# Grouped-query attention and a gated MLP: a fifth query buffer, fourth batch's query loads together, first v in halves

## The chip, the cores and the metric

The kernel runs on one core of a Trainium2 chip. The metric is the device time of one launch in microseconds: the median of several runs. A profiled execution gives the trace that the text reads; its span runs from the first to the last instruction. Engines: PE (TensorE), DVE (VectorE), ACT (ScalarE), POOL (GpSimd), SP (SyncE, here used for DMA issues alone).

## The reference

```python
B, Hq, Hkv, S, D = 8, 16, 4, 384, 64        # x is then B x 384 x 1024
k = np.repeat(k, 4, axis=1); v = np.repeat(v, 4, axis=1)
scores = np.matmul(q, k.transpose(0, 1, 3, 2)) / np.sqrt(D)
attn = softmax(scores)
x = np.matmul(attn, v).transpose(0, 2, 1, 3).reshape(B, S, 1024)

h = np.maximum(x @ w_in, 0.0)               # w_in 1024 x 1024
u, v = h[..., :512], h[..., 512:]
v_n = (v - mean(v)) / np.sqrt(var(v) + 1e-06)
v_s = np.einsum('ts,bsd->btd', w_spatial, v_n) + b_spatial[None, :, None]
out = (u * v_s) @ w_out                     # w_out 512 x 1024, out float32
```

All inputs are float32; the matmuls run in float16.

## The kernel before

The work is cut into 8 batches. A batch's attention has 18 units (`UNITS`): 6 sets (`SETS`, three tiles of 128 queries by two halves `j` of the heads) of 3 key tiles each. A unit's scores are two matmuls into PSUM (`units`, L277), ACT takes their exponential (`exp`, L289), and when a set's three units are through, PE multiplies with v (`weigh`, L297) and DVE divides by the row sums (L310, L312). The gated MLP of a batch follows behind as filler: `v_part` (L352), `u_part` (L411), the norm of v on POOL (`norm`, L396, results called vn), the spatial mixing `s_part` (L430, with DVE L442 and POOL L447), and `o_part` (L468, output stored by SP, L483). A generator (`gated`) hands it out matmul by matmul, with marks ("from", n) before which a part may not start; `pour` puts so much of it between the attention's units as a budget allows.

The order on each engine is that in which the program writes its instructions; the framework adds semaphore waits and nothing is reordered. A table `todo`, filled by `at(n, f, ...)`, calls loads, casts and transposes at unit n (the first 21 units are walked one by one, later ones three at a time: 21, 24, ... 36, 39, ...). So SP's queue is one list in program order: an instruction that waits holds all that stand behind it.

For each batch, q comes in two halves of 8 heads (`load_q`, L122, 768 KB each), k and v in one load each (`load_k`, `load_v`, L112, 384 KB). They land in float32 stage tiles from the pool `ld`: 4 rotating buffers for q (6 KB per partition each), 2 each for k and v. A tile's new load waits until the last reader of the tile that had the buffer before is done. POOL casts them to float16 (`cast_q` L200 to L205, `cast_k` L184, `cast_v` L188). For batches 0 and 1, PE transposes q and k (`q_turn` L237, `k_turn` L223); from batch 2 on, DMA does (`q_send` L255, `k_send` L247, results qT and kT), as it does for x (`x_send` L336, result xt, three sends per batch). PE reads qT and kT in the scores and xt in `v_part` and `u_part`.

At the start batch 0's loads are cut into parts that are spread over SP's and ACT's DMA queues (L141 to L149); `part_q(0, j, hs, ts, eng)` loads tiles `ts` of q's half `j`. A DMA's completion is told by one of 8 semaphores in rotation, so each SP or ACT load also waits until the one eight before it has landed. The third tiles follow later (`rest_q`). POOL casts v (`cast_v`, L585), issues weight loads and the loads of batch 1 (L586 to L592). The spatial weights and bias, `ws32` and `b32`, are constants of their own (L525, L526), loaded by SP (`load_spatial`), cast by POOL (`cast_spatial`) and transposed by DMA (L547).

From batch 3 on the same table rows serve each batch (L653 to L667), with two offsets `late` for batch 3. There the first q half is loaded at unit 38, the second at 40 (a step later); they are cast at 43 and 47 and transposed at 47 and 49.

Of the kernel before, what the change touches and what calls it, by code (L numbers as in the profile page):

```python
# [9 lines left out]
FP32 = mybir.dt.float32  # L10
# [7 lines left out]
def kernel(  # L18
# [15 lines left out]
    P = 128  # L34
    B, HQ, S, D = q.shape
    HKV = k.shape[1]
# [3 lines left out]
    NT = S // P  # L40
# [7 lines left out]
    UNITS = NT * SETS  # L48
# [4 lines left out]
    cst = ctx.enter_context(tc.tile_pool(name="cst", bufs=1))  # L53
    ld = ctx.enter_context(tc.tile_pool(name="ld", bufs=2))
# [12 lines left out]
            name=nc.get_next_instruction_name(), act_func_set_id=set_id, ins=[], outs=[]  # L67
        )
    )
    pool, dve, act, sp = nc.gpsimd, nc.vector, nc.scalar, nc.sync  # L70
# [32 lines left out]
    def stage_tile(n, b, j=None):  # L103
        shape = [P, 2, NT, G * D] if n == "q" else [P, HKV, NT * D]
        t = ld.tile(
            shape, FP32, name=f"{n}32_{b}_{j}", tag=f"{n}32", bufs=4 if n == "q" else 2
        )
        stage[n, b, j] = t
        return t

    def part(src, t, lo, hi, eng):
        eng.dma_start(t[:, lo:hi, :], src[lo:hi].rearrange("h (p t) d -> p h (t d)", t=NT))  # L112

    def load_k(b, eng=sp):
        part(k[b], stage_tile("k", b), 0, HKV, eng)

    def load_v(b, eng=sp):
        part(v[b], stage_tile("v", b), 0, HKV, eng)

    def part_q(b, j, hs, ts, eng):  # L120
        h0, h1, t0, t1 = hs[0], hs[-1] + 1, ts[0], ts[-1] + 1
        eng.dma_start(  # L122
            stage["q", b, j][:, h0:h1, t0:t1],
            q[b, 8 * j + 4 * h0 : 8 * j + 4 * h1].rearrange(
                "(h i) (c t r) d -> (i c) h t (r d)", i=G, t=NT, r=G
            )[:, :, t0:t1],
        )

    def load_q(b, j, eng=sp, ts=(0, 1, 2)):
        if ts[0] == 0:  # L130
            stage_tile("q", b, j)
        part_q(b, j, (0, 1), ts, eng)

    k0, v0, q00, q01 = (
        stage_tile("k", 0),
        stage_tile("v", 0),
        stage_tile("q", 0, 0),
        stage_tile("q", 0, 1),
    )
# [4 lines left out]
    part_q(0, 0, (1,), (0,), act)  # L144
    part(k[0], k0, 2, 4, sp)
    part_q(0, 1, (0, 1), (0,), act)
    part(v[0], v0, 0, HKV, sp)
    part_q(0, 0, (0, 1), (1,), act)
    part_q(0, 1, (0, 1), (1,), sp)  # L149

    w_in16 = cst.tile([P, NK, DFF], FP16, name="w_in16")
    w_out16 = cst.tile([P, NM, DM], FP16, name="w_out16")
# [5 lines left out]
    def load_w_in(half, lo, hi):  # L158
        cols = slice(half * DH, (half + 1) * DH)
        pool.dma_start(  # L160
            w_in16[:, lo:hi, cols],
            moe_w_in[lo * P : hi * P, cols].rearrange("(t p) f -> p t f", p=P),
        )
# [15 lines left out]
    def cast_k(b, eng, js=(0, 1), hs=slice(0, 2)):  # L179
        if b not in k16s:  # L180
            k16s[b] = ld.tile([P, 2, NT, 2, D], FP16, name=f"k16_{b}", tag="k16")
        src = stage["k", b, None].rearrange("p (j h) (t d) -> p j t h d", h=2, t=NT)
        for j in js:
            eng.tensor_copy(k16s[b][:, j, :, hs], src[:, j, :, hs])  # L184

    def cast_v(b, eng, js=(0, 1)):
        g0, g1 = 2 * js[0], 2 * js[-1] + 2
        eng.tensor_copy(  # L188
            v1[b % 2][:, g0:g1, :, 0:D].rearrange("p g t d -> p (g t) d"),
            stage["v", b, None][:, g0:g1].rearrange("p g (t d) -> p (g t) d", t=NT),  # L190
        )

    def cast_q(b, j, eng, ts=None, hs=(0, 1)):
        if (b, j) not in q16s:
            q16s[b, j] = ld.tile([P, NT, G, 2, D], FP16, name=f"q16_{b}_{j}", tag="q16", bufs=4)
        t16 = q16s[b, j]
        src = stage["q", b, j].rearrange("p h t (r d) -> p h t r d", d=D)
        for hh in hs:
            if ts is None:
                eng.tensor_copy(t16[:, :, :, hh, :], src[:, hh])  # L200
            elif len(ts) > 1:
                t = slice(ts[0], ts[-1] + 1)
                eng.tensor_copy(t16[:, t, :, hh, :], src[:, hh, t])
            else:
                eng.tensor_copy(t16[:, ts[0], :, hh, :], src[:, hh, ts[0]])  # L205
# [316 lines left out]
                yield from o_part(B - 1, tt, half)  # L522


    b32 = cst.tile([P, S], FP32, name="b32")  # L525
    ws32 = cst.tile([P, NT, S], FP32, name="ws32")  # L526
    ws16 = cst.tile([P, NT, NT, P], FP16, name="ws16")

    def load_spatial(eng):
        eng.dma_start(b32, moe_b_spatial.rearrange("(a s) -> a s", a=1).to_broadcast([P, S]))  # L530
        rows = moe_w_spatial.rearrange("(c t r) s -> r c t s", t=NT, r=G)
        for r in range(G):
            eng.dma_start(ws32[32 * r : 32 * r + 32], rows[r])

    def cast_spatial():
        pool.tensor_copy(
            bias_bc.rearrange("a (t r c) -> a t r c", t=NT, r=G),
            b32.rearrange("a (c t r) -> a t r c", t=NT, r=G),
        )
        for tt in range(NT):  # L540
            pool.tensor_copy(
                ws16[:, :, tt].rearrange("p s (r c) -> p s r c", r=G),
                ws32[:, tt].rearrange("p (c s r) -> p s r c", s=NT, r=G),
            )

    def send_spatial():
        sp.dma_start_transpose(  # L547
            wsT16.rearrange("p s (t c) -> p (s t) c", t=NT),
            ws16.rearrange("p s t c -> p (s t c)"),
        )  # L550
# [4 lines left out]
    def at(n, f, *args):  # L555
        todo.setdefault(n, []).append((f, args))
# [25 lines left out]
    q_turn(0, 0, 0, dve)  # L582
    idle(5)

    cast_v(0, pool)  # L585
    load_w_in(1, 4, 8)  # L586
    cast_q(0, 1, pool, (1,))
    load_k(1, pool)
    load_q(1, 0, pool)
    def behind_rest():  # L590
        load_q(1, 1, pool)
        load_v(1, pool)  # L592
        cast_q(0, 1, pool, (2,))
        load_w_in(0, 0, 4)
        load_w_in(0, 4, 8)
        pool.memset(b32[:, 0:1], 0.0)
        pool.memset(ws32[:, 0, 0:1], 0.0)
        load_spatial(sp)
        cast_k(1, pool)
        load_k(2, pool)  # L600
        cast_q(1, 0, pool)
        load_q(2, 0, pool, (0,))
        cast_q(1, 1, pool, (0,))
        cast_q(1, 1, pool, (1, 2))
        load_q(2, 1, pool, (0,))
        cast_v(1, pool)
        cast_spatial()
        send_spatial()

    at(3, behind_rest)  # L610
    at(2, idle, 6)
    at(2, cast_q, 0, 1, dve, (0,))
# [37 lines left out]
    for j, n in ((0, 34), (1, 36)):  # L650
        at(n, cast_q, 2, j, pool, (1, 2))
        at(n + 1, q_send, 2, j, 1, NT)
    for b in range(3, B):  # L653
        u0 = UNITS * b
        late = 6 if b == 3 else 0
        at(u0 - 24 + late, load_k, b)
        at(u0 - 24 + 2 * late, load_v, b)
        at(u0 - 22 + late, load_q, b, 0)
        at(u0 - 20 + late, load_q, b, 1)
        late = 3 if b == 3 else 0  # L660
        at(u0 - 16 + late, cast_k, b, pool)
        at(u0 - 14 + late, cast_q, b, 0, pool)
        at(u0 - 12 + late, k_send, b)
        at(u0 - 10 + late, q_send, b, 0)
        at(u0 - 10 + late, cast_q, b, 1, pool)
        at(u0 - 8 + late, q_send, b, 1)
        at(u0 - 4, cast_v, b, pool)  # L667

    STEP = (NT * NK * C512 + NM * NK * C384 + NM * NT * C384 + 6 * NM * C512) / SETS
# [48 lines left out]
    late = [(b, s, hh) for u in (ALONE, ALONE + 1) for b, s in ends.pop(u, []) for hh in range(2)]  # L718
    for n in range(ALONE, total, NT):
# [16 lines left out]
        late = []  # L736
# [41 lines left out]
```

## Time and profile before

| what | value |
|---|---|
| median of 3 runs | 241.75 us (241.71 to 242.37) |
| profiled execution | 242.33 us |
| its span | 240.4 us |
| granted PE clock | 0.999 |
| PE busy | 231.4 us |
| PE idle before 12 us | 3.4 us |
| PE idle from 12 to 68 us | 0.52 us |
| PE idle from 68 to 80 us | 1.24 us |
| PE idle from 80 to 236 us | 0 |

The profile's span is 1.9 us shorter than the time of the same execution. In the lists of instructions the columns are: start in us, duration in us (of all merged ones), engine (a q behind it: its queue of instructions, where DMA issues stand; PEld is PE's weight load), line, operation, what is written and read, count, and in brackets the engine's idle time before it and what ended it.

### The profile page before, as it was taken

The page shows a single profiled execution, that of the slowest core. Times are in us where ns is not written, and L with a number is a line of the kernel's source. Part 1 is how long each engine was busy: PE and PEld are TensorE (multiplying, and loading weights), DVE is VectorE, ACT ScalarE, POOL GpSimd, SP SyncE. Part 2 cuts the span into 40 slices and gives each one's busy share as a digit, 9 for nine tenths or more (in the row PEclk, how much of TensorE's full clock was granted, in tenths as well). Part 3 has the DMA queues.
Part 4 walks back from the last instruction along what each step waited for, and adds up shares of the span by engine and source line. Part 5 has one row for each costly group of instructions (what it writes and reads, how often), then busy time and mean ns, then how long its engine had stood idle before and what let it go on. Part 6 is the DMA issues. An engine that isn't in the chain of part 4 may idle for free.

```text
span 240.4 us, 5918 instructions
## 1 busy us (share of the span) xinstructions
PE 231.4 (96%) x2312; PEld 124.2 (52%) x2312; DVE 143.7 (60%) x379; ACT 169.9 (71%) x348; POOL 101.0 (42%) x144
## 2 busy tenths in 40 slices
PE   7799999999999899999999999999999999999993
PEld 6445566545555355554555445555455445545541
DVE  2577766566646666375844767366744767467362
ACT  2899997879897678977797776987587776501211
POOL 3768762553275540367025820556013500370540
PEclk9999999999999999999999999999999999999999
DMA  6999999999999999996988499939922534240157
GB/s 184 294 322 305 265 112 160 157 305 192 325 172 252 297 285 212 293 279 164 219 259 225 124 218 289 303 107 156 229 48 44 111 116 125 48 174 0 57 205 265
DMA packets 67451, 47.47 MB, mean 197 GB/s; under 512 B 48320, under 2 KB 60400, under 8 KB 67424
## 3 DMA queue, kind: packets, MB, share of 16 engines
q1 hardware_dynamic: 62496, 39.86, 68.8%
q0 software_dynamic: 3952, 6.42, 12.0%
q10 hardware_dynamic: 976, 0.82, 1.1%
q8 instruction: 18, 0.29, 0.5%
q14 instruction: 9, 0.07, 0.1%
HBM read 25.95 MB, written 12.58 MB: 160 GB/s over the span
## 4 chain that ended last, share of the span: by engine, by line
PE 90%; DMA 4%; DVE 3%; ACT 1%; POOL 1%; issue 0%; ACTq 0%
PE pu L411 18%; PE pv L352 17%; PE po L468 17%; PE sc L277 15%; PE av L297 14%; PE psp L430 7%; DMA q<-in_q_dram 3%; PE qps L237 1%; DMA k_None<-in_k_dram 1%; DVE x L312 1%; ACT aT L289 1%; POOL vn L396 1%; DVE osb L215 1%; PE xps L329 1%; DVE q L205 0%
## 5 line engine op out<-in xcount | busy, mean ns | idle before, releaser
L289 ACT ACTIVATE aT<-sc 128x512 f16<-128x512 f32 x288 | 148.0, 612 | 34.4 <-PE sc L277 33.3
L297 PEld LDWEIGHTS <-aT 128*128 128x128 f16 x1152 | 47.7, 97 | 16.9 <-issue 1.9
L297 PE MATMUL av<-v,aT 128*128 128x65 f16 x1152 | 51.5, 193 | 0.1
L352 PE MATMUL pv<-w_in,xt 128*128 128x512 f16 x192 | 50.8, 379 | 0.1
L468 PE MATMUL po<-w_out,gT 128*128 128x512 f16 (+2 forms) x196 | 50.5, 375 | 0.0
L411 PE MATMUL pu<-xt,w_in 128*128 128x384 f16 x256 | 49.9, 326 | 0.0
L396 POOL TENSOR_SCALAR vn<-vr,rstd,nmr 128x512 f16<-128x512 f32 x23 | 17.6, 779 | 71.6 <-DVE nmr L391 50.1
L447 POOL TENSOR_TENSOR gT<-vs,uT 128x384 f16<-128x384 f32 x31 | 32.4, 1057 | 30.9 <-DVE r L310 17.1
L277 PE MATMUL sc<-qT,kT 64*128 64x512 f16 x288 | 42.2, 380 | 1.2 <-DVE vs L442 0.9
L312 DVE TENSOR_TENSOR x<-av,r 128x256 f16<-128x256 f32 x96 | 40.7, 424 | 3.3
L310 DVE RECIPROCAL r<-av 128x4 f32<-128x4 f32 x96 | 17.1, 178 | 41.4 <-PE av L297 41.2
L215 DVE COPY osb<-po 128x512 f32<-128x512 f32 (+1 forms) x39 | 26.6, 682 | 17.3 <-PE po L468 17.3
L411 PEld LDWEIGHTS <-w_in 128*128 128x128 f16 x256 | 22.1, 97 | 17.1 <-issue 5.5
L422 ACT ACTIVATE uT<-pu 128x384 f16<-128x384 f32 x32 | 15.8, 493 | 16.3 <-PE pu L411 16.1
L468 PEld LDWEIGHTS <-gT 128*128 128x128 f16 x196 | 17.4, 97 | 17.2 <-issue 3.1
L352 PEld LDWEIGHTS <-xt 128*128 128x128 f16 x192 | 15.8, 97 | 17.9 <-issue 5.1
L277 PEld LDWEIGHTS <-kT 64*128 64x128 f16 x288 | 10.9, 94 | 25.8 <-issue 13.3
L430 PE MATMUL psp<-wsT,vn 128*128 128x384 f16 x96 | 22.4, 327 | 0.4 <-POOL vn L396 0.4
L200 POOL CAST q<-q 128x768 f16<-128x768 f32 x22 | 17.6, 830 | 10.8 <-DMA q<-in_q_dram 9.1
L442 DVE TENSOR_TENSOR vs<-psp,bias_bc 128x384 f32<-128x384 f32 x32 | 17.6, 551 | 7.3 <-PE psp L430 7.1
L366 DVE TENSOR_SCALAR vr<-pv 128x512 f32<-128x512 f32 x24 | 16.4, 681 | 8.5 <-PE pv L352 8.4
L378 DVE BATCH_NORM_STATS2 stats<-vr 128x6 f32<-128x512 f32 x24 | 16.4, 685 | 0.1
(47 smaller groups left out, 99.0 us busy)
## 6 DMA issues: line engine op xcount, KB each, us to landing
out_dram<-osb SPq DMA_DIRECT2D x21, 512.0 KB, 2.9
q<-in_q_dram SPq DMA_DIRECT2D x10, 768.0 KB, 7.7
v_None<-in_v_dram SPq DMA_DIRECT2D x7, 384.0 KB, 4.7
w_in<-in_moe_w_in_dram POOLq DMA_DIRECT2D x4, 512.0 KB, 11.2
k_None<-in_k_dram SPq DMA_DIRECT2D x5, 384.0 KB, 4.1
q<-in_q_dram POOLq DMA_DIRECT2D x2, 768.0 KB, 9.4
out_dram<-osb SPq DMA_DIRECT2D x5, 256.0 KB, 2.2
w_out<-in_moe_w_out_dram POOLq DMA_DIRECT2D x2, 512.0 KB, 7.5
```

The source lines that it names most:

```text
L200: eng.tensor_copy(t16[:, :, :, hh, :], src[:, hh])
L215: (act.copy if eng is act else dve.tensor_copy)(o, i)
L277: nc.tensor.matmul(sc, kTs[b][rows, j, kt * P : (kt + 1) * P], qTs[b, j][rows, qt].rearrange("p (r i c) -> p i r c", r=G, i=G), start=True ...
L289: act.activation(a, sc, AF.Exp, scale=scale)
L297: nc.tensor.matmul(av[:, i * (D + 1) : (i + 1) * (D + 1)], aT[:, kt, hh, i * P : (i + 1) * P], v1[b % 2][:, 2 * j + hh, kt, 0 : D + 1], st ...
L312: dve.tensor_tensor(x16s[b][:, qt, c : c + 256].rearrange("p (i d) -> p i d", i=G), o[:, :, 0:D], r.to_broadcast([P, G, D]), ALU.mult,)
L352: nc.tensor.matmul(pv, xts[b][:, kt, st * P : (st + 1) * P], w_in16[:, kt, DH:DFF], start=(kt == 0), stop=(kt == NK - 1),)
L396: (dve if b == 0 and st == 1 else pool).tensor_scalar(vn, v_r.pop((b, st)), rstd[:, st : st + 1], nmr[:, st : st + 1], op0=ALU.mult, op1=A ...
L411: nc.tensor.matmul(pu[:, 0:S], w_in16[:, kt, m * P : (m + 1) * P], xts[b][:, kt, :], start=(kt == 0), stop=(kt == NK - 1),)
L430: nc.tensor.matmul(psp[:, 0:S], v_n[b, st][:, m * P : (m + 1) * P], wsT16[:, st, :], start=(st == 0), stop=(st == NT - 1),)
L447: pool.tensor_tensor(gT, vs, uT, ALU.mult)
L468: nc.tensor.matmul(po[:, 0:width], gTs[b][:, m, tt * P : (tt + 1) * P], w_out16[:, m, c0 : c0 + width], start=(m == 0), stop=(m == NM - 1),)
```

## The change

The pool of q's float32 tiles has five buffers instead of four. The constants `b32` and `ws32` go; `new_spatial` takes one of the five buffers for both, just before they are loaded. Since buffers rotate, batch 4 and later use other ones than before.

At the start, v's load is cut into two halves of heads, with SP loading tile 1 of q's first half between them; tile 1 of q's second half goes to ACT's queue instead. POOL casts v in two parts accordingly, the second behind the cast of q's tile.

For batch 3, the two q loads stand one behind the other at unit 38 (an output's store comes behind both instead of between them); the second cast moves from 47 to 45 and its transpose from 49 to 47, one step of three units earlier. On SP's queue the second transpose now stands right behind the first, ahead of an x transpose and the loads of k and v of batch 4. All else keeps its place on each engine.

```diff
-            shape, FP32, name=f"{n}32_{b}_{j}", tag=f"{n}32", bufs=4 if n == "q" else 2
+            shape, FP32, name=f"{n}32_{b}_{j}", tag=f"{n}32", bufs=5 if n == "q" else 2
...
     part_q(0, 1, (0, 1), (0,), act)
-    part(v[0], v0, 0, HKV, sp)
-    part_q(0, 0, (0, 1), (1,), act)
-    part_q(0, 1, (0, 1), (1,), sp)
+    part(v[0], v0, 0, 2, sp)
+    part_q(0, 0, (0, 1), (1,), sp)
+    part_q(0, 1, (0, 1), (1,), act)
+    part(v[0], v0, 2, 4, sp)
...
-    b32 = cst.tile([P, S], FP32, name="b32")
-    ws32 = cst.tile([P, NT, S], FP32, name="ws32")
+    spatial32 = {}
+    def new_spatial():
+        t = ld.tile([P, NT + 1, S], FP32, name="spatial32", tag="q32", bufs=5)
+        spatial32["b"], spatial32["w"] = t[:, NT], t[:, 0:NT]
...
-    cast_v(0, pool)
+    cast_v(0, pool, (0,))
     load_w_in(1, 4, 8)
     cast_q(0, 1, pool, (1,))
+    cast_v(0, pool, (1,))
...
-        pool.memset(b32[:, 0:1], 0.0)
-        pool.memset(ws32[:, 0, 0:1], 0.0)
+        new_spatial()
+        pool.memset(spatial32["b"][:, 0:1], 0.0)
+        pool.memset(spatial32["w"][:, 0, 0:1], 0.0)
...
-    for b in range(3, B):
+    at(36, load_k, 3)
+    at(38, load_q, 3, 0)
+    at(38, load_q, 3, 1)
+    at(42, load_v, 3)
+    at(41, cast_k, 3, pool)
+    at(43, cast_q, 3, 0, pool)
+    at(45, k_send, 3)
+    at(46, q_send, 3, 0)
+    at(45, cast_q, 3, 1, pool)
+    at(47, q_send, 3, 1)
+    at(UNITS * 3 - 4, cast_v, 3, pool)
+    for b in range(4, B):
         u0 = UNITS * b
-        late = 6 if b == 3 else 0
...
```

More of the change, by code (lines that the diff above doesn't have):

```diff
@@ L522, in gated @@
                 yield from o_part(B - 1, tt, half)
-    b32 = cst.tile([P, S], FP32, name="b32")
-    ws32 = cst.tile([P, NT, S], FP32, name="ws32")
+    spatial32 = {}
+    def new_spatial():
+        t = ld.tile([P, NT + 1, S], FP32, name="spatial32", tag="q32", bufs=5)
+        spatial32["b"], spatial32["w"] = t[:, NT], t[:, 0:NT]
     ws16 = cst.tile([P, NT, NT, P], FP16, name="ws16")
     def load_spatial(eng):
+        b32, ws32 = spatial32["b"], spatial32["w"]
         eng.dma_start(b32, moe_b_spatial.rearrange("(a s) -> a s", a=1).to_broadcast([P, S]))
@@ L535, in cast_spatial @@
     def cast_spatial():
+        b32, ws32 = spatial32["b"], spatial32["w"]
         pool.tensor_copy(
@@ L652 @@
         at(n + 1, q_send, 2, j, 1, NT)
-    for b in range(3, B):
-        u0 = UNITS * b
-        late = 6 if b == 3 else 0
[L656 to L666, printed above, removed]
+    at(36, load_k, 3)
[10 more added lines that the diff above has]
+    for b in range(4, B):
+        u0 = UNITS * b
+        at(u0 - 24, load_k, b)
+        at(u0 - 24, load_v, b)
+        at(u0 - 22, load_q, b, 0)
+        at(u0 - 20, load_q, b, 1)
+        at(u0 - 16, cast_k, b, pool)
+        at(u0 - 14, cast_q, b, 0, pool)
+        at(u0 - 12, k_send, b)
+        at(u0 - 10, q_send, b, 0)
+        at(u0 - 10, cast_q, b, 1, pool)
+        at(u0 - 8, q_send, b, 1)
         at(u0 - 4, cast_v, b, pool)
```

## The prediction

> **What bounds the kernel now.** First the page's busy row and its DMA row (tenths of the 16 DMA engines in 40 slices of 6 us):
>
> ```profile
> PE 231.4 (96%) x2312; PEld 124.2 (52%) x2312; DVE 143.7 (60%) x379; ACT 169.9 (71%) x348; POOL 101.0 (42%) x144
> ...
> DMA  6999999999999999996988499939922534240157
> ```
>
> PE is the bound: 9.0 us of the 240.4 are idle. DMA is a second bound, but only in the first 18 slices (to 108 us). So next, where PE's idle time lies, by stages (columns: busy us and instructions of each engine, clock, DMA share, GB/s):
>
> ```profile
> 0.00:12.00 12.00, 8.60 (x102) 6.57 (x102) 4.77 (x18) 6.77 (x12) 6.51 (x18) 1.00 0.91 238
> 12.00:36.00 24.00, 23.64 (x306) 12.97 (x305) 17.77 (x55) 22.60 (x44) 17.85 (x32) 1.00 1.09 252
> 36.00:68.00 32.00, 31.84 (x349) 17.49 (x347) 19.49 (x55) 26.74 (x58) 11.68 (x16) 1.00 1.13 222
> 68.00:80.00 12.00, 10.76 (x111) 5.30 (x110) 6.78 (x17) 8.70 (x19) 9.08 (x12) 1.00 1.15 227
> 80.00:236.00 156.00, 156.00 (x1450) 81.54 (x1449) 93.93 (x236) 104.83 (x218) 55.85 (x69) 1.00 0.70 178
> ```
>
> From 80 to 236 us PE has no idle at all. A change can win only before 80 us: 3.40 us idle in the first stage, 0.36 and 0.16 in the next two, 1.24 in 68 to 80. Then the chain of waits for the first 12 us, and PE's own timeline for the rest:
>
> ```profile
> 3.08 6.58 DMA q<-in_q_dram
> ...
> 9.68 0.84 DVE q L205 x2
> ...
> 10.57 0.41 PE qps L237 x4
> ```
>
> ```profile
> 71.59 0.34 PE L430 MATMUL psp<-wsT,vn 128*128 128x384 f16 x1 [0.38 <-POOL vn L396]
> ...
> 79.05 0.82 PE L277 MATMUL sc<-qT,kT 64*128 64x512 f16 x6 [0.86 <-DVE vs L442]
> ...
> 88.15 0.61 PE L352 MATMUL pv<-w_in,xt 128*128 128x512 f16 x2
> ```
>
> The start hangs on the second tile (t=1) of the first q half: issued on ACT at 3.08, landed 9.66, cast by DVE to 10.5, transposed by PE at 10.57 after 1.40 us idle. At 71.59 PE waits 0.38 for `norm`'s vn; at 79.05 it waits 0.86. The row blames DVE there, but the weight loads of the same scores name the transposed q (`qT<-q`, 1.30 us), issued at 73.59 and 5.4 us to landing, so 79.0: the DMA ended it. Last, what POOL and SP's queue did around these two waits:
>
> ```profile
> 64.49 1.60 POOL L200 CAST q<-q 128x768 f16<-128x768 f32 x2 [4.65 <-DMA q<-in_q_dram]
> 67.69 1.60 POOL L200 CAST q<-q 128x768 f16<-128x768 f32 x2 [1.60 <-DMA q<-in_q_dram]
> 69.27 2.27 POOL L396 TENSOR_SCALAR vn<-vr,rstd,nmr 128x512 f16<-128x512 f32 x3
> ```
>
> ```profile
> 57.06 0.60 SPq L122 DMA_DIRECT2D q<-in_q_dram  x1
> 57.75 0.43 SPq L483 DMA_DIRECT2D out_dram<-osb  x1
> 58.28 0.38 SPq L122 DMA_DIRECT2D q<-in_q_dram  x1
> ...
> 70.16 2.16 SPq L336 DMA_TRANSPOSE xt<-x  x1
> ...
> 73.59 3.19 SPq L255 DMA_TRANSPOSE qT<-q  x1
> 76.88 1.05 SPq L122 DMA_DIRECT2D q<-in_q_dram  x2
> ...
> 78.53 3.37 SPq L336 DMA_TRANSPOSE xt<-x  x1
> ```
>
> The vn sit behind the cast of batch 3's second q half, whose load was issued behind an output; that half's transpose was issued behind xt, k and v.
>
> **The change, part by part.** The sum is made against the profiled execution (240.4 us span, 242.33 with what lies around it, 0.24% over the median of 241.75); its difference is then taken off the median.
>
> *The fifth buffer* costs and saves nothing. Two constants of 4 x 384 floats per partition become one tile of that size. It takes the new slot, so nothing is waited for; batch 4's first q half gets it next, loaded at 76.88, long after the last read (the weight casts, 27.57 + 2.46). Batch 4's second half takes the slot of q_2_0, last read at 51.41. Nothing is exposed if the slots turn out otherwise.
>
> *The start.* SP now issues v's first half, then the q tile (on ACT before), then v's second half; the second q half's tile moves to ACT, behind a wait for the first q load (landed 4.51) instead of the first k load (3.06). Instructions added: one DMA issue on SP (0.47 like its neighbours) and one POOL cast (0.83 becomes twice about 0.45, a 128x384 k cast being 0.50). In the trace the start's transfers land in the order of their issue (v 7.98, second half's tile 9.02, the tile in question 9.66), so I move them as one line: without the second v half (192 KB at 330 GB/s, v's own rate of 384 KB in 1.2 us: 0.6 us) and the 256 KB of the other tile it lands at about 8.3 (bounds: 8.0, and 9.66 if ACT's queue had not been slower). DVE is busy to 8.51, casts to 9.34, PE transposes at 9.39: 1.18 us earlier, of 1.40 idle. That is the most PE can win. But ACT computes exponentials almost without pause from 6.58 to 36: its idle time between 11.58 and 33.07 is 0.48 + 0.21 + 0.20 + 0.33 = 1.22 us, and PE can't outrun it. Part of each must stay: I take 0.8 (0 to 1.18).
> What is queued behind: ACT's copy of kT moves from 4.24 to about 4.95 and ends 5.43; the scores start at 6.17, when qT (6.12) is there, so 0.69 us of cover. POOL's cast of the second half's tile waits for the last landing (9.66), then v's second half to 11.0 (its first reader is at 13.89, or 12.7 once earlier); POOL's loads of k, q and v of batch 1 are issued 0.7 later, where the DMA engines are full anyway (share 1.19 in 12 to 16, 1.01 in 16 to 20), and the spatial weights likewise, whose transpose landed at 36.0 and is read at 44.05.
>
> *What of the 0.8 survives.* From 45.78 on SP's queue runs on landings and not on PE: load of q, cast (ends 51.41), transpose issued 51.43, 4.7 to landing, 56.18. The scores that read it started at 56.58. A PE that is 0.8 early stops there after 0.40. I keep 0.4 (0 to 1.0, if the transposes from 35.67 on get ahead of the w_out loads issued at 34.27 and the whole queue moves up).
>
> *Batch 3's second half.* Its load passes one output of 512 KB: 1.28 us by the landings 64.34 and 65.62, so it lands at 66.3 instead of 67.54, the cast ends at 67.9 and vn starts 1.4 us earlier: 0.38 gone, 0.78 in all. The next transposed q (issued 67.65, 5.6: 73.25) is read at 74.02, which allows 0.77. The output is 0.5 us later; its buffer is next written at 83.87. Its transpose passes xt, k4 and v4 and is issued near 70.2: lands near 74.5 for a reader at 78.2, 0.86 gone (the last of the six scores also waits for DVE's x, done at 77.94, so nothing stays). 0.77 + 0.86 = 1.63.
>
> *What is late next.* xt (b=2, second third), k4, v4 each go 1.5 to 2.4 us later, and both q of batch 4, an output and xt's last third (78.53) come behind them in one queue. That last third was issued at 78.53, 9.6 to landing: 88.1. PE's first reader ran at 88.15. There is no slack there at all, and x itself was ready at 77.94 or before, so the queue sets it. A PE that is 1.63 early waits for it. So the sum is this landing: qT to 72.4 (held as xt was, 2.2), xt to about 74.0 (such issues ended within 0.4 us after an earlier landing; here 73.25), k4 at 74.0 and 4.1 to landing: 78.1; v4 1.2 later: 79.3; from v to the second q 5.8 (next batch: v 96.34 + 4.4, q 97.46 + 9.1): 85.1; output 1.3, xt 0.8: **87.2**. Gain 88.15 - 87.2 = 0.95 us; after it PE has no idle to lose (next tight pair: transposed q landed 95.4, read at 99.6).
> Bounds: the q pair took 6.9 in this very place (79.0 to 85.9), and k4 may take v4's 4.7: 88.9 to 89.0. On the other side, each turn from loads to transposes shows a second in which DMA moved almost nothing (7 GB/s in 55 to 56, 6 in 70 to 71, 24 in 86 to 87), and the new order has one such turn less: up to 1 us, 86.2, past PE's own 1.63. At the removed turn the trace shows 195 and 203 GB/s (77 to 79), so I count nothing. [...]
>
> Profiled execution 242.33 - 0.95 = 241.4; on the median, 241.75 - 0.95 = **240.8**.
>
> **Rivals.**
> 1. *DMA keeps up*: the queue moves with PE, and all three stalls are won: 1.18 + 0.38 + 0.86 = 2.42, 239.3. For it: one turn less, and slack of 4 us after 88. Against: DMA share 1.09 to 1.15 in all of 12 to 80.
> 2. *Hidden anyway*: the same bytes pass before xt's last third, which lands at 88.1 as before; the stalls only move to 88: 241.75. For it: a saturated queue. Against: the near-empty seconds above, which a shorter queue of turns would not have.
> 3. *Slower*: k4 issued 1.6 us late, with the q pair at 6.9 and k4 at 4.7, puts xt's last third at 89.0; PE waits 0.85 longer than before: 242.6. It decides from a landing of 88.15 on. Against: the transpose that moved ahead took its own 1.3 us with it.
>
> **Chances.** Forecast 0.48 (its own range: landing 87.75 down to PE's 1.63, that is 240.1 to 241.35), rival 1 0.17, rival 2 0.19, rival 3 0.16. From no change this measurement can tell about 0.3%, 0.73 us. Of the forecast 0.38 lies beyond that: faster 0.38 + 0.17 = 0.55; same 0.10 + 0.19 = 0.29; slower 0.16. The range reaches into rivals 1 and 3, 239.4 to 242.5.
>
> **What would show it.** The first transposes after 10 us at about 9.4 instead of 10.57; ACT's pause of 0.48 near 12 gone; no wait at vn; the second half's transpose landing before its reader; and a new wait at `pv` near 87, behind xt. Wrong: PE without a wait at 85 to 89 (rival 1), a stall there past 88.2 (rival 3), a first tile that still lands after 9 us, or a new wait on kT before the first scores.

## The result and the profile after

The changed kernel takes 0.9926 of the time of the kernel before, 95% interval 0.9898 to 0.9953: medians of 240.06 and 242.21 us over 20 runs each, taken in turn. On the first median of 241.75 that is 240.0, a gain of 1.8 us. The quotient of the two medians, 0.9911, gives 2.15 us; the text goes by the ratio. Ratios leave out executions that lie more than 1.5% above the fastest of their kernel. The profiled executions differ by more, 242.33 against 239.56 (spans 240.4 and 237.5): the one before lies near its median, the one after among the fastest of its 20 runs. The runs of both kernels scatter by 3 us.

The stages of the changed kernel (columns as before: length, busy us of PE, PEld, DVE, ACT, POOL, clock, DMA share, GB/s):

```profile
0.00:12.00 12.00, 9.87 (x114) 7.35 (x114) 5.52 (x21) 7.14 (x14) 6.68 (x19) 1.00 0.93 242
12.00:36.00 24.00, 23.94 (x310) 13.21 (x310) 18.05 (x55) 22.10 (x45) 17.77 (x32) 1.00 0.99 255
36.00:68.00 32.00, 31.84 (x347) 17.44 (x345) 18.19 (x53) 27.74 (x60) 15.00 (x21) 1.00 1.10 238
68.00:80.00 12.00, 12.00 (x127) 6.11 (x124) 7.62 (x20) 9.64 (x20) 5.81 (x8) 1.00 1.05 241
80.00:233.00 153.00, 153.00 (x1416) 79.79 (x1415) 92.26 (x232) 102.31 (x212) 55.64 (x68) 1.00 0.69 176
```

PE's idle time falls from 3.40 to 2.13 us in the first stage, from 0.36 to 0.06 in the second, from 1.24 to nothing in 68 to 80. That is 2.81 of the 2.9 us between the two spans.

The start, in the chain of waits of the changed kernel:

```profile
8.42 0.61 PE sc L278 x4
9.03 0.34 PE qps L238 x4
9.37 0.02 issue
9.39 0.42 DVE qT L216
```

The q tile, issued on SP at 2.64, landed 4.9 us later, at 7.56 instead of 9.66. Its transposes follow the scores directly, 1.6 us earlier than before (8.96 against 10.57 in PE's timeline); PE no longer waits 1.40 us for them. Around the two later waits POOL and SP now show:

```profile
62.13 1.60 POOL L201 CAST q<-q 128x768 f16<-128x768 f32 x2 [3.46 <-DMA q<-in_q_dram]
64.19 1.60 POOL L201 CAST q<-q 128x768 f16<-128x768 f32 x2 [0.46 <-PE sc L278]
65.78 2.27 POOL L397 TENSOR_SCALAR vn<-vr,rstd,nmr 128x512 f16<-128x512 f32 x3
```

```profile
65.58 5.25 SPq L256 DMA_TRANSPOSE qT<-q  x2
70.92 1.26 SPq L337 DMA_TRANSPOSE xt<-x  x1
...
73.45 1.01 SPq L122 DMA_DIRECT2D q<-in_q_dram  x2
...
75.06 4.00 SPq L337 DMA_TRANSPOSE xt<-x  x1
```

The second cast follows the first with 0.46 us between them instead of 1.60, so vn starts at 65.8 instead of 69.3. Both transposes are one line (x2); the second was issued at 68.11 and took 4.2 us, so it lands at 72.3 for scores that start at 76.16. The last third of x is issued at 75.06 instead of 78.53 and takes 10.2 us: 85.25. PE's weight loads show how near that is:

```profile
85.29 0.11 PEld L353 LDWEIGHTS <-xt 128*128 128x128 f16 x2 [0.45 <-DMA xt<-x]
```

The load of weights waits 0.45 us for x, but the matmuls before it last until then: PE itself has no idle. The pair that had no slack before (88.11 and 88.15) has none now, 2.86 us earlier.

### The profile page after: what moved, and what is told of

Read it like the earlier page. It is cut to its first block, busy times and chain, and to the rows that moved or that the text cites. A ratio compares the mean times of both kernels' runs of the same rounds, so it can differ in the third digit from the quotient of the medians.

```text
span 237.5 us, 5921 instructions
## 1 busy us (share of the span) xinstructions
PE 231.4 (97%) x2312; PEld 124.3 (52%) x2312; DVE 142.8 (60%) x379; ACT 169.2 (71%) x348; POOL 100.9 (42%) x145
## 4 chain that ended last, share of the span: by engine, by line
PE 93%; DVE 3%; DMA 2%; ACT 1%; issue 0%; ACTq 0%
PE pu L412 18%; PE pv L353 18%; PE po L469 17%; PE sc L278 16%; PE av L298 15%; PE psp L431 7%; DMA q<-in_q_dram 2%; PE qps L238 1%; DVE x L313 1%; ACT aT L290 1%; DVE qT L216 1%; PE xps L330 1%; DVE osb L216 1%; PE kps L224 0%; DVE r L311 0%
## 5 line engine op out<-in xcount | busy, mean ns | idle before, releaser
L216 DVE COPY osb<-po 128x512 f32<-128x512 f32 (+1 forms) x39 | 26.5, 682 | 17.3 <-PE po L469 17.3
```

The source lines that it names most:

```text
L216: (act.copy if eng is act else dve.tensor_copy)(o, i)
```

## Experiments

Ratios are against the kernel before, with 95% intervals, from runs taken in turn on the same chip. Since single executions scatter, a second reading of each profile helps: the time at which PE starts the scores of a unit. Units 21, 54, 57 and 66 part the start, the way to the vn wait, the wait for batch 3's transposed q, and the wait for x's last third. After unit 66 all the kernels in the table take 148.9 to 149.0 us. The profiles of three more runs (e5, e6, e12), of executions that took 244 us and more, are not in the table.

```
us, from each kernel's trace       unit 21   21 to 54   54 to 57   57 to 66    span
kernel before                        29.27      44.75       5.03      12.33   240.4
changed kernel                       27.77      44.29       4.10      12.36   237.5
changed kernel, again (e4)           28.08      44.29       4.10      12.61   238.0
start alone (e1)                     28.65      44.39       5.38      12.31   239.7
batch 3 alone (e2)                   30.90      44.28       4.10      12.42   240.7
buffer alone (e3)                    30.17      44.53       4.57      12.31   240.6
changed, old load place (e7)         29.37      44.47       4.10      12.74   239.6
changed, old transpose place (e8)    28.03      44.28       5.44      12.54   239.2
the same, again (e11)                27.39      44.28       4.10      12.43   237.2
changed, batch 4's q later (e9)      28.65      44.29       4.10      12.34   238.3
changed, w_in early (e10)            28.39      45.67       4.10      12.62   239.7
```

**The parts alone.** First the start alone (the kernel before with these edits):

```diff
-    part(v[0], v0, 0, HKV, sp)
-    part_q(0, 0, (0, 1), (1,), act)
-    part_q(0, 1, (0, 1), (1,), sp)
+    part(v[0], v0, 0, 2, sp)
+    part_q(0, 0, (0, 1), (1,), sp)
+    part_q(0, 1, (0, 1), (1,), act)
+    part(v[0], v0, 2, 4, sp)
...
-    cast_v(0, pool)
+    cast_v(0, pool, (0,))
...
+    cast_v(0, pool, (1,))
```

> The kernel before with the start's new load order and v in halves alone. As forecast (DMA sets the pace from 45 us on): PE is 1.2 to 1.6 us early at 12 us, but stops again at the transposed q near 56 us and at vn and the transposed q near 71 and 79 us, so at most 0.4 us of it is left: ratio 0.998 to 1.000. Rival 'the queue moves along with PE' (as the trace after suggests): 1.4 us stay, ratio 0.994.

Measured: 0.9958 (0.9929 to 0.9987), median 241.22. That is between the two expectations, and the interval reaches both. PE's waits of more than 0.2 us after 12 us in its profile:

```profile
16.96 0.38 PE L353 MATMUL pv<-w_in,xt 128*128 128x512 f16 x1 [0.93 <-DMA w_in<-in_moe_w_in_dram]
78.41 0.82 PE L278 MATMUL sc<-qT,kT 64*128 64x512 f16 x6 [1.22 <-DMA qT<-q]
```

There is no wait near 56 us: where I had put the first cap, nothing stops PE. Two others do. `v_part` now reaches the second part of w_in's right half before it has landed (16.9 us), and at 78.4 the old place of batch 3's transpose costs 1.22 us, more than the 0.86 of before.

Then batch 3 alone (its new table rows in the kernel before), run in two sets:

```diff
+    at(38, load_q, 3, 0)
+    at(38, load_q, 3, 1)
...
+    at(45, cast_q, 3, 1, pool)
+    at(47, q_send, 3, 1)
```

> The kernel before with the new places of batch 3's second q half (load, cast, transpose) alone. As forecast: both waits near 71 and 79 us go (1.24 us), PE then waits for xt's last third near 87, 0.95 us stay: ratio 0.996. Rival 'the queue moves along': the whole 1.24 us, 0.995. Third: nothing, since the start's stall sets the rest: 1.000.

> Batch 3's new places alone, a second time, since its first profile shows both waits gone (span less the time of unit 21: 209.8 us, against 210.4 to 211.2 in kernels with the old places) while its ratio was 1.0007. If the 0.9 us between these sums is there in most executions, the ratio is 0.996 to 0.997 over both sets and the new profile has 209.7 to 210.3 again. If a late start hides the old transpose's landing in most executions, so that batch 3's part pays only behind the new start: 0.999 to 1.001 again.

Measured: 1.0007 (0.9974 to 1.0040) and 0.9993 (0.9961 to 1.0025). The profile of the first shows what the edit is meant to do, 44.28 and 4.10 us in the table against 44.75 and 5.03, both waits gone; no gain shows in the times. The profile of the second set has 44.41 and 4.10 us there too, but its span less the time of unit 21 is 210.6 us, above what was expected, with 0.70 us of wait for x's last third at 90.76. The first set's profiled execution started late (unit 21 at 30.90). The buffer alone started late too (30.17), with the old places, and it lost less at them than the kernel before did:

```profile
72.27 0.34 PE L430 MATMUL psp<-wsT,vn 128*128 128x384 f16 x1 [0.15 <-POOL vn L396]
79.27 0.82 PE L277 MATMUL sc<-qT,kT 64*128 64x512 f16 x6 [0.41 <-DVE osb L215]
```

0.56 us here, 1.24 in the kernel before: PE that comes 0.9 us later finds more of the transfers landed. So in these executions with the old start the two waits are worth less than one profile says. That this explains the whole of the missing gain is not shown; 1.24 us would be 0.995, below both intervals. The clock, further down, explains a part.

The buffer alone is the changed kernel with the start and batch 3 put back:

```diff
-    part(v[0], v0, 0, 2, sp)
+    part(v[0], v0, 0, HKV, sp)
...
-    at(38, load_q, 3, 1)
+        at(u0 - 20 + late, load_q, b, 1)
```

> The changed kernel with the old start and the old batch 3: only the fifth q buffer is left, lent to the spatial weights and bias. Both theories: nothing, ratio 1.000 (0.997 to 1.003); PE's three waits stand as in the profile before. If the ratio is below 0.997, the buffer carries part of the gain, and the sum was wrong to leave it at nothing.

Measured: 1.0021 (0.9981 to 1.0061). It carries nothing, as forecast. The changed kernel itself, unedited, beside its parts:

> The changed kernel itself, beside its parts on the same chip: 0.9926 was measured (0.990 to 0.995). If the gains of the parts add up to this one, nothing was lost between them; if start and batch 3 alone give less than half each, they need each other, as 'DMA sets the pace' has it.

Measured: 0.9938 (0.9891 to 0.9986), median 240.07. The parts give 0.42%, nothing and nothing, together 0.42% against 0.62 to 0.74%; the intervals allow both a plain sum and a part that pays only in company.

**The granted clock.** The mean clock granted to PE is on record for every execution of the experiments, and none lies between 0.993 and 0.996. Of the executions that enter the ratios, 32 of 127 with the old start (kernel before, batch 3 alone, buffer alone) have 0.993 or less, and 1 of 92 with the whole new start. In the kernel before these take 1.2 us more than the others (means 243.06, 19 runs, and 241.87, 74 runs). The first profile of batch 3 alone is one of them:

```profile
11.37 0.61 PE L237 MATMUL qps<-ident,q 128*128 128x128 f16 x4 [1.89 <-DVE q L205]
12.00:13.00 1.00, 1.00 (x23) 1.00 (x21) 0.72 (x3) 0.00 (x0) 1.00 (x2) 0.50 0.82 129
```

PE waits 1.89 us for the q tile; near the end of that wait the clock falls to 0.5 for 3.4 us, and four transposes take 0.61 us instead of 0.40. The four profiles with such a fall (e2, e5, e6, e12) all have a PE wait of 1.5 to 2.5 us just before it. But a wait of 1.97 us in the profile of the buffer alone is followed by none, so it is not shown that the wait causes the fall. The plain ratios of batch 3 alone hold 9 such executions of 22. Without them, a comparison made only afterwards, batch 3 alone is 0.47 us below the kernel before, give or take 0.48; the start alone is 0.76 below (0.54 either way) and the changed kernel 1.24 (0.92). So the parts may well add up, and by an estimate (1.2 us in 19 of 93 runs) about 0.2 us of the gain is lower clock that no longer comes.

**What in the start counts.** The queues exchanged with v in one piece, and v in halves with the queues as they were:

```diff
     part(v[0], v0, 0, HKV, sp)
-    part_q(0, 0, (0, 1), (1,), act)
-    part_q(0, 1, (0, 1), (1,), sp)
+    part_q(0, 0, (0, 1), (1,), sp)
+    part_q(0, 1, (0, 1), (1,), act)
```

> The kernel before, v in one piece, with the two q tiles exchanged between SP's and ACT's queues alone. If transfers land in the order of their issue, the q tile lands behind all of v (8.0 us) at about 8.7: the first transposes at about 9.6 instead of 10.6, 1.0 us early, of which the old batch 3 lets about 0.6 through: ratio 0.997. If v's halves are what counts: 1.000.

```diff
-    part(v[0], v0, 0, HKV, sp)
+    part(v[0], v0, 0, 2, sp)
     part_q(0, 0, (0, 1), (1,), act)
     part_q(0, 1, (0, 1), (1,), sp)
+    part(v[0], v0, 2, 4, sp)
```

> The kernel before with v's load and cast in halves alone, the q tiles on their old queues (ACT's one behind its wait for the first k load). In the order of issue the q tile passes v's second half only: about 9.1 instead of 9.7, so 0.6 us early at most, ratio 0.998. If the halves carry the start's gain: 0.996 as for the whole new start.

(The second edit also casts v in halves on POOL, as the whole new start does.) Measured: queues 0.9936 (0.9907 to 0.9966), halves 0.9976 (0.9926 to 1.0026). The exchange of queues alone does as much as the whole new start within the intervals, and more than the 0.997 expected; v's halves alone show no gain that can be told from none, from six executions. The profiles agree: with the queues exchanged PE waits 0.14 us for the tile's transposes (at 9.72), with v in halves alone 2.45 us (at 11.85).

**What in batch 3 counts.** The changed kernel with the second load back behind the output's store, and with the second transpose back behind xt, k4 and v4 (twice):

```diff
-    at(38, load_q, 3, 1)
+    at(40, load_q, 3, 1)
```

> The changed kernel with batch 3's second q load back behind the output's store (unit 40), its cast and transpose at the new places. The load lands about 1.3 us later, so does vn; the transposed q has 3.8 us to spare in the trace after (landed 72.3, read at 76.2): at most 0.4 us is lost, ratio 0.993 to 0.995. If the pair of loads is the point of it: 0.996.

```diff
-    at(47, q_send, 3, 1)
+    at(49, q_send, 3, 1)
```

> The changed kernel with batch 3's second transpose back at its old place (unit 49), behind an x transpose and the loads of k and v of batch 4. By the theory that an early start runs into this landing, as it did with the start alone (78.4 us, 1.2 us of wait): 0.996. If the start's gain is held back by something else, no loss: 0.993.

> The changed kernel with batch 3's second transpose at its old place, a second time, for more runs and another profile: the first had 1.27 us of wait at this transposed q in its profile (a 241.3 us execution), yet a ratio of 0.9917. If the wait is in all executions, the ratio is 0.996 over both; if only in executions whose transfers run late, it is 0.992 again and a fast execution shows the landing before its reader.

Measured: load 0.9934 (0.9904 to 0.9964); transpose 0.9917 (0.9885 to 0.9949) and 0.9943 (0.9917 to 0.9969). Neither loses anything that can be measured against the changed kernel's 0.9926 and 0.9938, though the first profile of the old transpose has this:

```profile
16.33 0.38 PE L353 MATMUL pv<-w_in,xt 128*128 128x512 f16 x1 [0.77 <-DMA w_in<-in_moe_w_in_dram]
...
77.74 0.82 PE L278 MATMUL sc<-qT,kT 64*128 64x512 f16 x6 [1.27 <-DMA qT<-q]
```

and the second, a faster execution, has this at the same place:

```profile
75.46 0.38 PE L353 MATMUL pv<-w_in,xt 128*128 128x512 f16 x1
75.77 0.85 PE L278 MATMUL sc<-qT,kT 64*128 64x512 f16 x6
```

No bracket, no wait. The transpose was issued at 70.3 there and landed 5.4 us later, at 75.7; in the first it was issued at 72.2 and landed at 77.7. The same program: in one execution its transfers are 2 us earlier and the old place costs nothing, in the other it costs 1.27. So this edit can pay only in executions whose transfers run late; how often they do is not known, and the ratios show no gain from it. The one profile that I forecast from held such a loss.

**What ends it now.** Batch 4's q loads put behind x's last third on SP's queue:

```diff
-        at(u0 - 22, load_q, b, 0)
-        at(u0 - 20, load_q, b, 1)
+        at(u0 - (18 if b == 4 else 22), load_q, b, 0)
+        at(u0 - (18 if b == 4 else 20), load_q, b, 1)
```

> The changed kernel with batch 4's two q loads four and two units later, so that on SP's queue they stand behind x's last third of batch 2 instead of ahead of it. The forecast had this landing as what ends the gain (85.25 us in the trace after, read at 85.29). If it holds time back, x lands about 4 us earlier, the small waits there (0.2 to 0.3 us in other executions) go, and the ratio is 0.990 to 0.992. If nothing waits there any more: as the changed kernel, 0.993.

Measured: 0.9917 (0.9886 to 0.9948). x's last third lands at 82.3 instead of 85.25 and units 57 to 66 take 12.34 us; in the changed kernel 12.36 and 12.61, with the old load place 12.74. So this landing costs between nothing and 0.4 us from one execution to the next. The time does not tell the two apart.

Last, the second part of w_in's right half issued at once:

```diff
     load_w_in(1, 0, 4)
+    load_w_in(1, 4, 8)
...
     cast_v(0, pool, (0,))
-    load_w_in(1, 4, 8)
```

> The changed kernel with the second part of w_in's right half issued right behind the first (near 4.6 us, where POOL is idle) instead of behind v's first cast (7.3 us). Theory: an early start now ends at this landing (16.0 us in the trace after, read at 16.08; 0.8 to 1.5 us of wait there in three of the profiles since), and this makes the upper group of times (241.2 to 241.8): it goes, median 239.5, ratio 0.988 to 0.991. Rival: the loads of the third q tiles (landed 12.1 and 14.3) share the engines with it and land later, PE waits for these instead: 0.993 or above.

Measured: 0.9955 (0.9926 to 0.9984), median 241.28: above the changed kernel's figures, though the intervals overlap, and at the rival's value. PE no longer waits for w_in in its profile. But issued at 4.5 instead of 7.3 us, it landed at 16.0 all the same; the third q tiles landed at 13.5 and 17.3 instead of 12.1 and 14.3, POOL, which waits for them in its order, fell behind by up to 4 us (w_out issued at 36.8 instead of 33.1), and a cast of v came too late for PE:

```profile
53.01 0.54 PE L298 MATMUL av<-v,aT 128*128 128x65 f16 x12 [1.17 <-POOL v L189]
```

No version beat the changed kernel beyond the intervals.

## Why the prediction was right or wrong

The direction and the range held, and the size was between the forecast (0.95 us) and the first rival (2.42), nearer to the rival: 240.0 lies just outside the forecast's own range of 240.1 to 241.35. One of its own signs of being wrong came too, PE without a wait at 85 to 89 us (in the second profile 0.20 us). That the range held is owed to the rival inside it. The fall of PE's waits sums up, by the table, to 1.50 before unit 21, 0.46 to unit 54 and 0.93 to unit 57: 2.89 in the two profiles, of which the runs keep about 1.8.

*The start: right in kind, too small in size.* I took 0.8 of at most 1.18 us; 1.50 came. The tile landed at 7.56, not 8.3, and the ceiling that I set from ACT was too low. I summed the pauses that the timeline names (0.48 + 0.21 + 0.20 + 0.33). But a merged line hides shorter ones. ACT before, and after:

```profile
6.58 5.00 ACT L289 ACTIVATE aT<-sc 128x512 f16<-128x512 f32 x10 [1.87 <-PE sc L277]
12.07 10.87 ACT L289 ACTIVATE aT<-sc 128x512 f16<-128x512 f32 x20 [0.48 <-PE sc L277]
```

```profile
6.62 14.83 ACT L290 ACTIVATE aT<-sc 128x512 f16<-128x512 f32 x30 [1.69 <-PE sc L278]
```

Twenty exponentials took 10.87 us, 0.54 each, where ten before them took 0.50 each; after the change thirty run without a break at 0.49. So 20 x 0.05 = 1.0 us of ACT's slack stood inside that line, and with the named pause of 0.48 it makes the 1.5 us that were won.

*What survives: wrong, the step that failed.* I kept 0.4 us, because I read SP's queue from 45.78 on as paced by landings alone, with 0.40 us between the transposed q and its scores as a cap. Before, and after:

```profile
51.43 1.23 SPq L255 DMA_TRANSPOSE qT<-q  x1
```

```profile
48.69 1.23 SPq L256 DMA_TRANSPOSE qT<-q  x1
```

It landed at 52.35 instead of 56.18, before scores at 55.08. The queue moved along: its list begins with an x transpose that waits for PE's and DVE's work (34.17 instead of 35.67), POOL issued w_out at 33.09 instead of 34.27, and all behind followed. But the landing moved by 3.8 us, more than the 1.5 that PE won: the cap itself was one draw. In the other profiles, old start or new, that transposed q lands 2.5 to 3.4 us before its scores, whether these begin at 54.7 or at 59.8; only with w_in moved are there 0.18 us. In every profile of the table, except the one that moved w_in, units 21 to 54 take 44.3 to 44.8 us however early they begin. A queue that is full between two points can still start earlier, here by 1.50 us.

*Batch 3: both waits went, as computed* (0.46 and 0.93 against 0.38 and 0.86), with the transpose landing at 72.3 for the 74.5 forecast. Their worth did not hold as a sum: with the old transpose the wait ranged from nothing to 1.3 us between executions, and the plain ratios of this part alone show nothing; at full clock it is 0.47 us, give or take 0.48. The forecast took one execution's stall as the kernel's.

*What is late next: the right place, the wrong time.* x's last third is the transfer that PE meets with no slack. It was forecast at 87.2 and came at 85.25. The 2 us arose ahead of it: the second transposed q was issued at 68.11 for the 70.2 of the sum; from k4's landing on the sum was right (9.1 us forecast, 9.3 measured). It costs 0 to 0.4 us, not the 0.7 that I charged.

*Fifth buffer and cover at the start: right.* The buffer alone is 1.0021 within its interval, and ACT's later copy of kT (4.45) never held the scores, which started at 6.21.

*Readings.* The forecast's near-empty "seconds" are stretches of one microsecond, and one of them was not idle: at 70 to 71 us 6 GB/s moved, but the DMA share is 0.92 (0.06 and 0.13 in the other two). The transposed spatial weights are first read at 43.88, not 44.05, which changes nothing. That an x transpose's issue ends within 0.4 us after an earlier landing, which the sum used for xt, did not hold in the changed kernel: the one at 70.92 ended at 72.18, 1.12 us after the last landing ahead of it (71.06).

*The rivals.* "DMA keeps up" was right in its mechanism: its three stalls (1.40, 0.38 and 0.86 us in the trace before) went. "Hidden anyway" and "slower" fell by the interval. What I did not see: the next wait of an earlier start, w_in's second part at 16 to 17 us, and that the granted clock differs between the executions of the two starts.

## What to carry to other kernels

Before a queue is called the bound, look at what its first entry in that stretch waits for: if that is the engine you speed up, the queue can come along (here from 35.67 to 34.17 us). Read slack from the mean duration inside merged lines too, not only from named pauses (0.54 against 0.49 us per exponential here). And where a landing meets its reader within a microsecond, one profile gives one draw of that wait (1.27 us and nothing for the same program here), so compare two or three profiles before its length goes into a sum. Look at the granted clock of every run as well: an edit that pays can hide behind a few executions at a lower one (batch 3 alone had 9 of 22 at 0.993 or less).

## What was not expected of the hardware

At the start the order of issue over SP's and ACT's queues was the order of landing in both profiles, as the forecast took it: in the kernel before the loads issued at 2.13, 2.64 and 3.08 landed at 7.98, 9.02 and 9.66, in the changed kernel the tile issued at 2.64 landed at 7.56, v's second half (3.16) at 8.12, the tile on ACT (4.03) at 9.05. It is no rule: in the first profile of batch 3 alone the load issued on SP at 2.63 landed at 10.37, behind the one issued on ACT at 3.08 (9.79). An earlier issue did not help the w_in load from POOL's queue: at 4.5 and at 7.3 us it landed at 16.0. The landings of one and the same program differed by up to 2 us at 75 us between executions, at a granted clock of 0.999 to 1.000. What makes an execution's transfers early or late stays open.
